# Attention, a Fourier mix and a feed-forward network on one core: three V slots, borrowed buffers, one batch's Fourier transform in f32, and a new order of the work

## The chip, the cores and the metric

The kernel runs on one core of one Trainium2 chip. The metric is the device time of one execution in microseconds (us); lower is better. The engines are TensorE (PE: matmuls and transposes; its weight loads are shown apart as PEld), VectorE (DVE), ScalarE (ACT), GpSimd (POOL) and SyncE (SP), which issues most of the DMA transfers.

## The reference

Eight batches of 576 positions, eight heads of 64. Attention sees a band of 64 positions; its output x is mixed by the real part of a two-dimensional Fourier transform, normalised, and run through a feed-forward network (512 to 2048 to 512) without biases:

```python
scores = (1 / sqrt(D)) * (q @ k.T)
mask = (rel >= 0) & (rel < 64)
attn = softmax(where(mask, scores, -1e9))
x = (attn @ v)                          # B x S x (H * D) = 8 x 576 x 512
u = x + real(fft(fft(x, axis=1), axis=2))
un = (u - mean(u)) / sqrt(var(u) + 1e-6)
out = u + relu(un @ w_ch1) @ w_ch2      # the weights come as 64-bit floats
```

## The kernel before, in words

**Tiles.** The 4,608 positions are 36 tiles T of 128 rows; nine tiles are a pair of batches. `attn_tile` loads K, Q and V of a tile, brings K and Q into transposed form, takes the scores of each 64-row half against its own and the previous 64 keys, subtracts the row minimum of the negated scores (DVE, tile `nm`), exponentiates (ACT, tile `pr`, the "P buffers"), transposes P (tile `pt`), multiplies with V (tile `pa` in PSUM) and normalises half a tile at a time into `xu` (`normed`, on DVE or on ACT as four activations). Then a radix-4 step over the columns and a transpose (`py`) collect a batch's rows in `yT`.

**Plain and split.** Tiles with T < `PRO` = 13 are "whole": they compute in f32, with PE transposes. Later ones are "split": each f32 number is a sum of two f16 numbers, and a product takes the three passes of `PASSES` (high x high, high x low, low x high); their transposes are DMA transposes. The first feed-forward chunk (`PLAIN` = 1) is in f32, the other 17 in split f16.

**Fourier transform.** `fft(b)` folds `yT` (DVE or POOL), forms three sums f and three h, splits each into high and low (`part`, `rest`), runs the first transform on PE against the constants `dd` (`dstage`, tiles `pg`, then `g`), the second against `ds_` (`sstage`, tile `pz`), mixes the two sides (`odd` on ACT, `mix` on DVE, tile `mp`) and sends the rows to memory (`send`). For batch 0 alone the rows of tiles 0 and 1 also go straight to the tiles `mt` (`direct`, 12 transfers). `norm_tile` gathers the rows (`mt`), adds them to `xu`, normalises and transposes into the FFN's input `uhl`.

**Weights.** 32 pieces of 512 KB (`weight_piece`) are loaded as 64-bit floats, made into f32 by three DVE operations, squared on ACT for a scale, and later split by `weight_split`. `Bwl` is a mark that all loads write, so that each load stands after the one before it.

**FFN.** `ffn(c)` takes two tiles at a time through 16 steps; each has a first product (`ph`, in the PSUM banks `f1`), ReLU on ACT and the remainder on DVE (`hh`), and a second product (`po`, in the two banks `f2`).

**The order.** No loop order decides what runs when. Every step is an `op` with an engine, an assumed duration, the buffers it reads and writes and a priority; `Plan.order` walks through a model of the engines, lets each take the ready step with the best start and priority, and the steps are issued in that order, each engine's queue then running in order. `RINGS` holds how many buffers of a kind there are. The tables `NUDGE`, `LEAD` and `BIAS` shift priorities and the choice between two engines, per kind of step, per place and per tile. Ahead of the first FFN matmul, wherever the model has PE waiting for more than 0.8, fill-in matmuls (`warm`) are issued, which compute nothing that is used:

```python
if early and o.eng == "PE" and gap > WARM[0]:
    for _ in range(int((gap - WARM[1]) / 0.21)):
        nc.tensor.matmul(warm, wide[:, 0:P], wide, start=True, stop=True)
```

**V.** Each 64-row half needs the keys' values of its own 64 rows and of the 64 before. Before, there are two buffers `va` for a tile's own rows and two `ve` for the rows before them; `v_own` copies the tile's upper half into its `ve` and `v_next` its lower half into the next tile's `ve`, two SBUF-to-SBUF transfers a tile (lines 624 and 632).

Of the kernel before, what the change touches and what calls it, by code (L numbers as in the profile page):

```python
# [12 lines left out]
F32 = mybir.dt.float32  # L13
F16 = mybir.dt.float16
# [39 lines left out]
PLAIN = 1  # L54
W_DMA, W_DMA_STEP, W_CONV, W_SQ, W_SPLIT, W_STEP = -30, 1.0, 40, 110, 60, 0.3
NUDGE = {
    "": (
        4.8, -0.5, 0, 4.7, -0.4, 23.1, 1.2, 18.3, -6.3, 3.3, 12.7,
    ),
    "even": (  # L60
# [12 lines left out]
    ),  # L73
    "part": (
        3, -3.6,
    ),
    "piece": (
        3.8, 0, -4.9, -12.5,
    ),
    "scale": (  # L80
        -7.5, -1.8, 30.2, 0, -0.8,
    ),
    "split": (
# [3 lines left out]
    ),  # L87
    "whole": (
        -1.6, -1.5, 14.9, 5.2, 0, 32.4, -0.2, 12.7, 3.6, -0.7, 0, -1.8, 0.6, 53.2, 1.4, -2,
        0, 0.4, -1.3, -1.6, -36.8, 3.3, -0.3, 5, 1.5, -1.3, -4.4, 0, -12.1, 2.1,  # L90
    ),
# [1342 lines left out]
```

## Time and profile before

| what | value |
|---|---|
| median of 3 runs | 999.92 us (998.57 to 1003.39) |
| the profiled execution, its own time | 1001.33 us |
| its span, first to last instruction | 999.6 us |
| mean granted clock of TensorE | 0.997 of full speed |
| busy: PE, DVE, ACT, POOL | 973.2, 678.3, 413.9, 158.9 us |
| matmul records, fill-in among them | 9083, 105 |
| data moved by DMA | 123.63 MB |

How to read it: busy time is the time in which an engine has an instruction running, over the whole span. Matmuls are pipelined and their ends are modelled, so a busy PE isn't PE at its peak. The "granted clock" is the share of TensorE's full speed. A wait is put down to what came last before the waiting instruction started. An f32 matmul that isn't a transpose makes two records in the trace, so 64 records are 32 matmuls.

### The profile page before, as it was taken

The page shows a single profiled execution, that of the slowest core. Times are in us where ns is not written, and L with a number is a line of the kernel's source. Part 1 is how long each engine was busy: PE and PEld are TensorE (multiplying, and loading weights), DVE is VectorE, ACT ScalarE, POOL GpSimd, SP SyncE. Part 2 cuts the span into 40 slices and gives each one's busy share as a digit, 9 for nine tenths or more (in the row PEclk, how much of TensorE's full clock was granted, in tenths as well). Part 3 has the DMA queues.
Part 4 walks back from the last instruction along what each step waited for, and adds up shares of the span by engine and source line. Part 5 has one row for each costly group of instructions (what it writes and reads, how often), then busy time and mean ns, then how long its engine had stood idle before and what let it go on. Part 6 is the DMA issues. An engine that isn't in the chain of part 4 may idle for free.

```text
span 999.6 us, 23005 instructions
## 1 busy us (share of the span) xinstructions
PE 973.2 (97%) x9083; PEld 684.4 (68%) x9083; DVE 678.3 (68%) x1810; ACT 413.9 (41%) x1141; POOL 158.9 (16%) x179
## 2 busy tenths in 40 slices
PE   8788999999999999999999999999999999999998
PEld 6666767676676667766676666766676667666664
DVE  4689898877878667787885578786875645542121
ACT  5667666755344344443452244442454212121111
POOL 0002101024112231231111221131013100200000
PEclk9999999999999999999999999999999999999999
DMA  9988975235647684878762575868665401330000
GB/s 212 225 216 214 238 198 131 67 70 125 136 118 166 139 161 99 182 163 147 156 120 67 124 176 110 177 123 159 130 139 113 95 12 45 58 71 23 1 22 22
DMA packets 310955, 123.63 MB, mean 124 GB/s; under 512 B 292728, under 2 KB 292856, under 8 KB 310848
## 3 DMA queue, kind: packets, MB, share of 16 engines
q1 hardware_dynamic: 308128, 113.25, 51.6%
q0 software_dynamic: 2720, 8.92, 3.4%
q8 instruction: 71, 1.16, 0.5%
q14 instruction: 36, 0.29, 0.1%
HBM read 54.99 MB, written 14.17 MB: 69 GB/s over the span
## 4 chain that ended last, share of the span: by engine, by line
PE 84%; DMA 6%; DVE 5%; ACT 2%; SPq 1%; issue 1%; POOL 0%; DVEq 0%; ACTq 0%; POOLq 0%
PE ph L1325 35%; PE po L1306 34%; PE pa L765 3%; PE pg L1001 2%; PE pz L1033 2%; PE psc L655 2%; DMA kn<-in_k 1%; DMA pt<-flex 1%; DMA mt<-md,gix 1%; DMA flex<-in_moe_w_ch 1%; PE warm L1405 1%; PE psc L669 1%; PE py L869 1%; PE pp L713 1%; DVE hh L1343 1%
## 5 line engine op out<-in xcount | busy, mean ns | idle before, releaser
L1325 PE MATMUL ph<-uhl,w0s 128*128 128x256 f16 (+1 forms) x3384 | 427.1, 277 | 3.8 <-DVE hh L1343 2.3
L1306 PE MATMUL po<-w1s,hh 128*128 128x512 f16 (+1 forms) x1696 | 425.9, 387 | 0.0
L1325 PEld LDWEIGHTS <-w0s 128*128 128x128 f16 x3264 | 317.5, 98 | 90.8 <-issue 8.0
L1340 ACT ACTIVATE hh<-ph 128x256 f16<-128x256 f32 x272 | 104.3, 384 | 423.4 <-PE ph L1325 351.2
L1343 DVE SCALAR_TENSOR_TENSOR hh<-ph,hh 128x256 f16<-128x256 f32 x272 | 114.6, 422 | 223.5 <-ACT hh L1340 203.1
L1306 PEld LDWEIGHTS <-hh 128*128 128x128 f16 x1632 | 155.7, 98 | 138.3 <-issue 0.2
L698 ACT ACTIVATE pr<-pr,nm 128x128 f32<-128x128 f32 x184 | 58.2, 392 | 4.0 <-DVE nm L689 4.0
L1135 POOL TENSOR_TENSOR rs<-mv,mhalf 128x1 f32<-128x1 f32 x36 | 23.6, 657 | 202.8 <-DVE mv L1131 190.8
L1111 POOL DMA_INDIRECT mt<-md,gix x34 | 37.3, 1098 | 100.9 <-DMA md<-mp 86.2
L727 POOL TENSOR_TENSOR flex<-pr,flex 128x512 f16<-128x512 f32 x27 | 33.5, 1242 | 110.5 <-ACT flex L491 69.9
L568 POOL TENSOR_TENSOR flex<-kn,flex 128x512 f16<-128x512 f32 x23 | 29.2, 1271 | 122.4 <-ACT flex L491 74.8
L780 ACT ACTIVATE xu<-pa,rc 128x64 f32<-128x64 f32 x152 | 35.0, 321 | 28.8 <-DVE rc L773 16.4
L689 DVE CUSTOM_DVE_ANT_0 pr<-psc,mskb 128x128 f32<-128x128 f32 x184 | 41.7, 284 | 2.8 <-PE psc L655 1.8
L765 PE MATMUL pa<-ve,pt 128*64 128x65 f16 (+1 forms) x760 | 39.7, 205 | 3.4 <-ACT pr L698 1.7
L765 PE MATMUL pa<-va,pt 128*64 128x65 f16 (+1 forms) x760 | 39.7, 205 | 0.6 <-DMA pt<-flex 0.5
L698 ACT ACTIVATE pr<-psc,nm 128x128 f32<-128x128 f32 x104 | 28.8, 387 | 6.4 <-DVE nm L687 6.2
L1033 PE MATMUL pz<-g,ds__76 97*96 97x257 f16 (+3 forms) x240 | 29.0, 273 | 0.5 <-DVE mp L1055 0.5
L1033 PEld LDWEIGHTS <-ds__76 97*96 97x96 f16 (+1 forms) x240 | 26.6, 124 | 2.5 <-DVE mp L1055 0.6
L655 PEld LDWEIGHTS <-qbd 128*64 128x64 f16 x736 | 21.6, 110 | 9.1 <-issue 9.0
L655 PE MATMUL psc<-kst,qbd 128*64 128x128 f16 x736 | 27.3, 221 | 0.0
L579 DVE TENSOR_TENSOR flex<-qn,flex 128x1024 f16<-128x1024 f32 x22 | 26.8, 1219 | 0.2
L1363 DVE SCALAR_TENSOR_TENSOR xu<-po,osc,xu 128x512 f32<-128x512 f32 x34 | 23.8, 742 | 3.7 <-PE po L1306 3.7
(162 smaller groups left out, 1121.8 us busy)
## 6 DMA issues: line engine op xcount, KB each, us to landing
wd<-in_moe_w_ch SPq DMA_DIRECT2D x20, 512.0 KB
out<-xu SPq DMA_DIRECT2D x36, 256.0 KB
ve<-va SPq DMA_DIRECT2D x67, 130.0 KB
kn<-in_k SPq DMA_DIRECT2D x32, 256.0 KB
qn<-in_q SPq DMA_DIRECT2D x32, 256.0 KB
flex<-in_moe_w_ch SPq DMA_DIRECT2D x12, 512.0 KB
flex<-in_v SPq DMA_DIRECT2D x20, 256.0 KB
md<-mp SPq DMA_DIRECT2D x24, 192.0 KB
```

What stands on the lines that cost most here:

```text
L655: nc.tensor.matmul(t["ps", x][64 * j : 64 * j + 64, hp], qbd[i][:, j, h, 64 * z : 64 * z + 64], keys(h, j), start=(z == 0), stop=(z == 1),)
L689: nc.vector.tensor_tensor_reduce(out=t["pr", jj][:, hp], in0=t["ps", jj][:, hp], in1=mskb[:, m : m + P], scale=-0.125, scalar=3.0e38, op0= ...
L698: nc.scalar.activation(pr, src, AF.Exp, bias=t["nm", jj][:, hp : hp + 1], scale=-1.0)
L727: eng.tensor_tensor(out=pp[:, :, 1], in0=t["pr", jj], in1=pp[:, :, 0], op=ALU.subtract)
L765: nc.tensor.matmul(pa[half_, hh], pt, v_, start=(x == 0), stop=(x == len(mm) - 1))
L780: nc.scalar.mul(xv[:, hh], pa[:, hh, 0:64], rc[:, hh])
L1033: nc.tensor.matmul(pz[:M, c0:c1], ds_[:NJ, a, c[0] : c[0] + c[1]], t["g", gi][:, b_, c0:c1], start=(x == 0), stop=(x == len(mm) - 1),)
L1111: nc.gpsimd.indirect_dma_start(out=mts[T], out_offset=None, in_=mds[pb][0 : HR if n < 4 else 2 * HR], in_offset=bass.IndirectOffsetOnAxis( ...
L1306: nc.tensor.matmul(t["po"][i], l_, r_, start=(f == 0 and x == 0), stop=(f == NKF - 1 and x == len(mm) - 1))
L1325: nc.tensor.matmul(ph, l_, r_, start=(x == 0), stop=(x == len(mm) - 1))
L1340: nc.scalar.activation(t["hh", f][:, 0], ph, AF.Relu)
L1343: nc.vector.scalar_tensor_tensor(out=hh[:, 1], in0=ph, scalar=0.0, in1=hh[:, 0], op0=ALU.max, op1=ALU.subtract)
```

## The change

- **V in three slots.** Tile T uses slot T mod 3 for its own rows. The slot of the tile before keeps its lower half and gets the new tile's upper half (`v_own`), and is then the `ve` of tile T: one copy a tile.
- **A second home for P.** For odd whole tiles the two P buffers and their two transposes lie in four sections of `flex` (`apart`), where weight pieces were loaded before; weight pieces now use `flex` only in one of its three pairs of sections (every fifth piece, before three of every seven).
- **Attention in the FFN's PSUM banks.** For T < `FREE` = 5 the product with V goes to `f2`.
- **K and Q.** Three buffers instead of two; tiles 1, 2 and 4 borrow those of `mp` and `g` (`KQ_AT`).
- **Batch 0's Fourier transform in f32.** `constants` adds the two f16 parts of `dd` and `ds_` into f32 tiles; `dstage` and `sstage` then take one f32 matmul in place of three f16 ones, and the splits into high and low are left out.
- **`direct`** is issued by ACT instead of SP.
- **Weight loads unchained:** a load no longer stands after the one before it; the mark `Bwl` is still read by what must come after all of them.
- **Order:** tile 5 counts among the early ones (`CUT`), new values in all tables, smaller `PATIENT`.

```diff
+FREE = 5
+KQ_AT = {1: "mp", 2: "g", 4: "mp"}
+CUT = 5
 NUDGE = {
     "": (
-        4.8, -0.5, 0, 4.7, -0.4, 23.1, 1.2, 18.3, -6.3, 3.3, 12.7,
+    "": {0: -0.7, 1: 2.2, 3: -9.2, 4: 11, 5: 2.6, 6: 0.1, 7: 1.1, 8: -3.1, 9: 10, 10: 1.3, 11: -1.3},
...
-    PATIENT = {"DVE": 0.25, "ACT": 0.5, "POOL": 0.75, "DMA": 0}
+    PATIENT = {"DVE": 0.1, "ACT": 0.25, "POOL": 0.75, "DMA": 0}
...
-        "kq": 2, "pr": 2, "pt": 2, "xu": XR, "y": 1, "yT": 1, "tail": 1,
+        "kq": 3, "pr": 2, "pt": 2, "xu": XR, "y": 1, "yT": 1, "tail": 1,
...
-    vbuf = [cp.tile([P, H * 65], F32, name=f"v{x}{i}") for x in "ae" for i in range(2)]
+    vbuf = [cp.tile([P, H * 65], F32, name=f"v{x}") for x in range(3)]
...
+        own, old = T % 3, (T + 1 if T == PRO else T - 1) % 3
...
         def v_own():
-            nc.sync.dma_start(vbuf[2 + i][0:64], vbuf[i][0:64])
-
-        def v_next():
...
-                nc.sync.dma_start(vbuf[3 - i][64:128], vbuf[i][64:128])
+            nc.sync.dma_start(vbuf[old][0:64], vbuf[own][0:64])
...
+        apart = whole and T % 2
+        prs = Bfl[0:2] if apart else [Buf("pr"), Buf("pr")]
...
+            at_ = "f2" if T < FREE else "ps"
+            bpa = Buf(at_)
...
+    def constants():
...
+                eng.tensor_tensor(out=whole_c[x], in0=src[:, 0, c0 : c0 + n], in1=src[:, 1, c0 : c0 + n], op=ALU.add)
+
+            op("POOL", 0.9, -39 + 0.01 * x, add, [Bdd if x < 2 else Bds], [Bc[x]], alt=("DVE", 0.45))
...
+        plain = b == 0
...
+                if plain:
+                    bfh[nm, r] = b3[r]
+                    continue
...
+                    for x, (s_, qq, c) in enumerate(terms if plain else ()):
...
+                        nc.tensor.matmul(to, s_[:, qq], w_, start=(x == 0), stop=(x == n - 1))
...
-                            nc.sync.dma_start(mts[T][r0 : r0 + 3 * (a1 - a0) - 2 : 3], t["mp", cl][a0:a1])
+                            nc.scalar.dma_start(mts[T][r0 : r0 + 3 * (a1 - a0) - 2 : 3], t["mp", cl][a0:a1])
...
-        w, more = {}, order % 7 - 4 if order % 7 > 3 else None
+        w, more = {}, 2 if order % 5 == 4 else None
...
-        op("DMA", 1.75, W_DMA + W_DMA_STEP * order, load, writes=[*bw, Bwl], lat=2.5)
+        Bwl.writers.append(op("DMA", 1.75, W_DMA + W_DMA_STEP * order, load, writes=bw, lat=2.5))
...
-        base = PITCH * T + (LATER if T > 4 else -EARLY)
+        base = PITCH * T + (LATER if T > CUT else -EARLY)
```

**Where the order moves.** First SP's queue near its start (`kn`, `qn`, `va` or `v`: loads of K, Q and V; `ve<-va` or `v<-v`: the copies; `wd`: a weight piece; `dd`: Fourier constants). Before:

```order
L516 DMA va0_81<-in_v 128x8x64
L516 DMA va1_82<-in_v 128x8x64
L516 DMA kn2_145<-in_k 128x8x64
L516 DMA qn2_172<-in_q 128x8x64
L632 DMA ve1_84<-va0_81 64x520
L624 DMA ve0_83<-va0_81 64x520
L453 DMA dd_75<-in_dft_d 128x1536
L516 DMA kn1_206<-in_k 128x8x64
L516 DMA qn1_221<-in_q 128x8x64
L624 DMA ve1_84<-va1_82 64x520
L1204 DMA wd0_0_249<-in_moe_w_ch1 128x1024
L632 DMA ve0_83<-va1_82 64x520
```

And with the change:

```order
L610 DMA v2_83<-v0_81 64x520
L497 DMA v1_82<-in_v 128x8x64
L497 DMA kn2_185<-in_k 128x8x64
L497 DMA qn2_198<-in_q 128x8x64
L497 DMA kn3_227<-in_k 128x8x64
L497 DMA qn3_244<-in_q 128x8x64
L497 DMA kn4_269<-in_k 64x8x64 x2
L610 DMA v0_81<-v1_82 64x520
L497 DMA v2_83<-in_v 128x8x64
L497 DMA qn4_329<-in_q 64x8x64 x2
L1238 DMA wd0_0_355<-in_moe_w_ch1 128x1024
```

Before, the first weight piece stands ahead of K and Q of tiles 3 and 4, and each tile has two copies; with the change K and Q of tiles 0 to 4 stand ahead of it, and each tile has one copy. Up to the load of K of tile 11, which PE needs just ahead of the first FFN matmul, SP issues with the change 17 weight pieces, 32 tiles' worth of K, Q or V and 8 copies.

Next the twelve `direct` transfers (`mt<-mp`). Before, they are in SP's queue:

```order
L1078 DMA mt0_1178<-mp0_1_1099 32x512
L1078 DMA mt0_1178<-mp0_1_1099 11x512
L1078 DMA mt1_1208<-mp0_1_1099 32x512
L1078 DMA mt1_1208<-mp0_1_1099 10x512
L1204 DMA flex_79<-in_moe_w_ch2 128x1024
L1061 DMA md0_1256<-mp0_1_1099 96x512
```

With the change they stand in ACT's queue between other work (`g`: the copy of the first transform's result; `pr`: exponentials; `mp`: one side of the mix):

```order
L1081 COPY mp0_2_962<-pz0_2_961 96x2
L1110 DMA mt1_998<-mp0_1_946 32x512
L1110 DMA mt1_998<-mp0_1_946 10x512
L1110 DMA mt0_1007<-mp0_1_946 32x512
L1110 DMA mt0_1007<-mp0_1_946 11x512
L471 ACTIVATE g0_0_985<-pg0_0_984 97x512
L471 ACTIVATE yT1_877<-py5_1010 128x4x128
L694 ACTIVATE pr6_0_911<-psc6_0_912,nm6_0_972 128x128 x4
```

A weight piece and the transfer to memory no longer stand behind them on SP; the copy for the third part of the transform, and the exponentials of tile 6, stand behind them on ACT.

Last DVE's queue in batch 0's Fourier transform, before (`fs`, `hs`: the split f16 numbers):

```order
L945 SCALAR_TENSOR_TENSOR f1_0_900<-f0_0_780,xe0_750 128x388
L950 TENSOR_TENSOR f0_0_780<-f0_0_780,xe0_750 128x388
L969 TENSOR_TENSOR fs1_0_905<-f1_0_900,fs1_0_905 128x388
L969 TENSOR_TENSOR fs0_0_907<-f0_0_780,fs0_0_907 128x388
L941 TENSOR_TENSOR h2_0_944<-yT0_298 128x388
L945 SCALAR_TENSOR_TENSOR h1_0_949<-h0_0_833,yT0_298 128x388
L950 TENSOR_TENSOR h0_0_833<-h0_0_833,yT0_298 128x388
```

And with the change:

```order
L960 SCALAR_TENSOR_TENSOR h1_0_852<-h0_0_760,yT0_377 128x388
L965 TENSOR_TENSOR h0_0_760<-h0_0_760,yT0_377 128x388
L960 SCALAR_TENSOR_TENSOR f1_0_862<-f0_0_734,xe0_701 128x388
L767 TENSOR_SCALAR rc5_0_890<-pa5_0_867 128x4
L770 RECIPROCAL rc5_0_890<-rc5_0_890 128x4
L965 TENSOR_TENSOR f0_0_734<-f0_0_734,xe0_701 128x388
```

The remainders `fs` and `hs` are gone; four additions for the f32 constants stand a little earlier in the queue. On PE, the fill-in matmuls ahead of the first FFN matmul are 62 in 12 runs where they were 105 in 19. Over the whole program ACT normalises 58 halves of attention output where it had 38, and DVE 14 where it had 34.

## Rows read from the trace of the kernel before

**Rows 1.** Stage: its us, busy PE, PEld, DVE, ACT, POOL, clock, DMA share, GB/s:
```profile
0.00:103.00 103.00, 85.40 (x1051) 68.72 (x1052) 74.02 (x169) 66.43 (x208) 7.95 (x21) 0.97 0.89 219
103.00:180.00 77.00, 76.96 (x543) 54.25 (x542) 66.80 (x144) 46.48 (x129) 7.77 (x7) 1.00 0.68 176
180.00:995.00 815.00, 810.33 (x7493) 561.47 (x7491) 536.18 (x1497) 301.01 (x806) 143.13 (x151) 1.00 0.50 107
```
**Rows 2.** The chain that ended last, by engine, whole span:
```profile
PE 84%; DMA 6%; DVE 5%; ACT 2%; SPq 1%; issue 1%; POOL 0%; DVEq 0%; ACTq 0%; POOLq 0%
```
**Rows 3.** Groups by line, PE, 0 to 102.76 us (busy us, mean ns, idle before):
```profile
L1405 PE MATMUL warm<-ident 128*128 128x256 f16 x105 | 17.8, 315 | 1.4 <-POOL va L457 1.4
```
**Rows 4.** PE's waits, 0 to 102.7 us (us in total, times, longest):
```profile
PE pk L553 <- DMA kn<-in_k: 2.1, 2, 1.9
PE pq L553 <- ACT xu L780: 1.9, 1, 1.9
```
**Rows 5.** Pieces of the chain of waits (start us, us, what):
```profile
30.13 2.68 PE py L869 x24
...
57.45 4.59 PE py L869 x24
...
67.53 1.13 PE pa L765 x32
...
70.35 2.12 PE pg L1001 x48
...
102.92 1.73 PE ph L1325 x8
...
164.58 2.63 PE pz L1033 x24
```
**Rows 6.** Timeline of SP, the twelve `direct` transfers (start us, us):
```profile
77.80 3.53 SPq L1078 DMA_DIRECT2D mt<-mp  x4
...
82.43 2.78 SPq L1078 DMA_DIRECT2D mt<-mp  x4
...
86.33 2.80 SPq L1078 DMA_DIRECT2D mt<-mp  x4
```
**Rows 7.** Busy time in two short stretches, columns as in rows 1:
```profile
56.00:60.00 4.00, 3.20 (x17) 2.97 (x18) 3.93 (x7) 3.67 (x14) 0.00 (x0) 0.71 0.82 216
...
75.00:100.00 25.00, 20.53 (x254) 15.98 (x253) 23.50 (x61) 18.30 (x65) 5.33 (x7) 0.93 0.82 215
```
**Rows 8.** Groups by line, DVE, 0 to 102.7 us:
```profile
L1011 DVE SCALAR_TENSOR_TENSOR g<-pg,g 97x512 f16<-97x512 f32 x3 | 2.0, 684 | 0.0
...
L969 DVE TENSOR_TENSOR fs<-f,fs 128x388 f16<-128x388 f32 x3 | 1.7, 562 | 0.1
L969 DVE TENSOR_TENSOR hs<-h,hs 128x388 f16<-128x388 f32 x3 | 1.6, 556 | 0.0
```
**Rows 9.** DMA, 0 to 103 us (issues: line, KB each):
```profile
DMA packets 38449, 22.57 MB, mean 219 GB/s; under 512 B 34051, under 2 KB 34179, under 8 KB 38436
...
wd<-in_moe_w_ch SPq DMA_DIRECT2D x12, 512.0 KB
flex<-in_moe_w_ch SPq DMA_DIRECT2D x7, 512.0 KB
...
ve<-va SPq DMA_DIRECT2D x17, 130.0 KB
```
**Rows 10.** Groups by line, ACT, 180 to 995 us:
```profile
L1340 ACT ACTIVATE hh<-ph 128x256 f16<-128x256 f32 x270 | 103.6, 384 | 422.3 <-PE ph L1325 351.2 <-PE po L1306 46.2 <-DVE hh L1343 18.7
...
L780 ACT ACTIVATE xu<-pa,rc 128x64 f32<-128x64 f32 x88 | 20.3, 319 | 14.7 <-DVE rc L773 9.0 <-PE pa L765 3.1 <-DVE rc L770 2.5
```
**Rows 11.** PE's waits, 103 to 996 us:
```profile
PE ph L1325 <- DVE hh L1343: 2.3, 6, 0.8
PE ph L1325 <- ACT hh L1340: 1.3, 2, 0.7
```

More of the change, by code (lines that the diff above doesn't have):

```diff
@@ L231, in op @@
         o = Op()
-        shift, lead = NUDGE.get(self.kind, ()), LEAD.get({"split": "whole", "odd": "even"}.get(self.kind, self.kind), ())
-        prio += (shift[self.k] if self.k < len(shift) else 0.0) + (lead[self.at] if self.at < len(lead) else 0.0)
+        lead = LEAD.get({"split": "whole", "odd": "even", "first": "even"}.get(self.kind, self.kind), ())
+        prio += NUDGE.get(self.kind, {}).get(self.k, 0.0) + (lead[self.at] if self.at < len(lead) else 0.0)
         o.group = (self.kind, self.at, self.k)
@@ L441, in attn_fft_ffn_kernel @@
     Bid, Bmh, Bmskb, Bgix, Bdd, Bds, Bones = (Buf() for _ in range(7))
-    Bq, Bva, Bve = ([Buf() for _ in range(2)] for _ in range(3))
+    Bq = [Buf() for _ in range(2)]
+    Bv = [[Buf(), Buf()] for _ in range(3)]
     BkT = [Buf() for _ in range(3)]
@@ L619, in attn_tile @@
         if not whole:
-            op("ACT", 0.52, base + 3, lambda: v_part(0), [bv], [Bva[i]])
-            op("DVE", 0.6, base + 3.1, lambda: v_part(1), [bv], [Bva[i]])
+            op("ACT", 0.52, base + 3, lambda: v_part(0), [bv], Bv[own])
+            op("DVE", 0.6, base + 3.1, lambda: v_part(1), [bv], Bv[own])
         def v_own():
-            nc.sync.dma_start(vbuf[2 + i][0:64], vbuf[i][0:64])
-        def v_next():
-            if T + 1 == PRO:
-                (hi, lo), v_ = (ve[1 - i][64:128, z] for z in range(2)), va32[i][64:128]
+            nc.sync.dma_start(vbuf[old][0:64], vbuf[own][0:64])
@@ L629, in v_next, with v_tail @@
+        was = plan.k
+        if T == PRO:
+            last = (T - 1) % 3
+            plan.begin("tail", T)
+            plan.k = 1
+            def v_tail():
+                (hi, lo), v_ = (va[old][64:128, z, :, 0:64] for z in range(2)), va32[last][64:128, :, 0:64]
                 nc.vector.tensor_scalar(out=hi, in0=v_, scalar1=VS, scalar2=None, op0=ALU.mult)
                 nc.vector.scalar_tensor_tensor(out=lo, in0=v_, scalar=VS, in1=hi, op0=ALU.mult, op1=ALU.subtract)
-            else:
-                nc.sync.dma_start(vbuf[3 - i][64:128], vbuf[i][64:128])
@@ L634, in attn_tile @@
-        op("DMA", 0.55, base - 4 if whole else base + 3.2, v_own, [Bva[i]], [Bve[i]], lat=2.8)
-        if n + 1 < NT and T + 1 == PRO:
-            op("DVE", 1.1, base + 6, v_next, [Bva[i]], [Bve[1 - i]])
-        elif n + 1 < NT:
-            op("DMA", 0.55, base - 3.9 if whole else base + 6, v_next, [Bva[i]], [Bve[1 - i]], lat=2.8)
+            if n == 0:
+                op("POOL", 0.7, base - 25, lambda: nc.gpsimd.memset(va[old][64:128, :, :, 0:64], 0.0), writes=[Bv[old][1]])
+            else:
+                op("DVE", 1.1, base + 0.3, v_tail, [Bv[last][1]], [Bv[old][1]])
@@ L640, in attn_tile, with quarter @@
+            part_ones(last)
+            plan.begin("split", T)
+        plan.k = was
+        op("DMA", 0.55, base - 4 if whole else base + 3.2, v_own, [Bv[own][0]], [Bv[old][0]], lat=2.8)
         m = P * (1 if n == 0 else 2 if n == 4 else 0)
         banks = [Buf("ps"), Buf("ps")]
-        prs = [Buf("pr"), Buf("pr")]
+        apart = whole and T % 2
+        prs = Bfl[0:2] if apart else [Buf("pr"), Buf("pr")]
         rd = [Bq[i], bkT, *([] if n == 0 else [BkT[before]])]
+        def quarter(x):
+            return flex[:, x].rearrange("p (a s) -> p a s", a=4)
@@ L743, in attn_tile, with av @@
         Bx[T] = bx
-        vts = (ve32[i], va32[i]) if whole else (ve[i], va[i])
+        vts = [(va32 if whole else va)[x] for x in (old, own)]
         for hf in range(2):
-            bpa = Buf("ps")
-            def av(hf=hf):
+            at_ = "f2" if T < FREE else "ps"
+            bpa = Buf(at_)
+            def av(hf=hf, at_=at_):
                 if hf == 0:
                     xts[T] = sb([P, DM], F32, "xu", f"xu{T}")
-                pa = t["pa", hf] = bank("ps", f"pa{T}_{hf}", (P, 4, 65))
+                pa = t["pa", hf] = bank(at_, f"pa{T}_{hf}", (P, 4, 65))
                 for hh in range(4):
@@ L930, in fft @@
             b1, b0_ = low[0][bsrc], low[-1][bsrc]
-            b3 = [Buf("r3") for _ in range(3)]
+            r3 = "fh" if plain and x else "r3"
+            b3 = [Buf(r3) for _ in range(3)]
             def view(src):
```

181 lines of the change are left out of this document (98 added, 83 removed), and 10 rows, old and new, of the table NUDGE.

## The prediction

> **What bounds the kernel now.** I first read TensorE's share of the span by stage, then the chain of waits, then each engine's waits inside the first stage. TensorE (PE in the rows) is busy for 76.96 of 77 us from 103 to 180 us and for 810.33 of 815 us from 180 to 995 us [rows 1], and the chain that ended last is 84% PE [rows 2]. So after about 103 us the time is the sum of PE's work, and whatever is saved must either be PE work or lie before 103 us, where the feed-forward part (FFN) starts: its first matmul on PE's queue begins close to 102.9 us [rows 5]. Until 103 us PE is busy for 85.40 us, so it idles for 17.6 us [rows 1], and of its busy time 17.8 us are the 105 fill-in matmuls that the program sets wherever its order foresees a gap, and that compute nothing [rows 3]. Together 35.4 us of the first 103 us are no work. The idle part has many small causes, none over 2.1 us in total: loads of keys, then a normalisation on ACT, and so on down [rows 4]. Behind them DVE is busy for 23.50 of 25 us from 75 to 100 us and ACT for 18.30 [rows 7], and the DMA engines move 22.57 MB by 103 us, 219 GB/s [rows 9]. No single engine bounds this stage: it is a chain through PE, ACT, DVE and the loads, with all of them nearly full towards its end.
>
> A measurement of this kernel can tell about 0.5% (5 us) from no change. The profiled execution took 1001.33 us, its span 999.6 us plus 1.7 us around it; the median of the runs is 999.92 us, 1.4 us lower. The sum is made against 1001.33 us, and 1.4 us is taken off at the end.
>
> **The change part by part.**
>
> *Fewer fill-in matmuls.* The changed order has 62 of them ahead of the first FFN matmul where there were 105, in 12 runs instead of 19; the first three runs (18, 2 and 2) are the same. One costs 17.8 / 105 = 0.17 us [rows 3], so 43 fewer are 7.3 us less on PE. **-7.3 us**, certain as work, but only gone from the time if no wait takes its place; that is the next term.
>
> *Idle time around them.* PE idled for 17.6 us in this stage [rows 1]; 1.4 us of it is the start [rows 3], the same in both. The other 16.2 us lay around 16 runs of fill-in, and the change has 9 such runs. In proportion to the runs 16.2 x 7/16 = 7.1 us go. What removes them is visible in the order: the loads for tiles 0 to 4 now stand ahead of the first weight load on SP, since keys and queries have a third buffer and three borrowed homes, so that PE's 2.1 us of waits for keys [rows 4] should go; P buffers of odd tiles and the attention output of tiles 0 to 4 no longer queue for the same slots. Bounds: by the matmuls themselves (83 to 40 after the common start) 16.2 x 43/83 = 8.4 us go; if all waits only move, 0. I take **-7.1 us**, since a run marks a wait better than its length does.
>
> *Batch 0's Fourier transform in f32.* It had 72 matmuls for the first transform and 30 for the second, in three f16 passes: 2.12 x 72/48 = 3.2 us and 2.63 x 30/24 = 3.3 us, 6.5 us on PE [rows 5]. In f32 there are 24 and 10, with 2,304 and 2,560 columns. Wide f32 matmuls cost 1.73 us for 4 of 256 columns, 1.69 ns a column; the narrow f32 ones of the attention output cost 1.13 us for 8 pairs of 65 columns, 2.2 ns a column [rows 5]. The f32 transform so takes 4,864 x 1.69 = 8.2 us to 4,864 x 2.2 = 10.7 us, 1.7 to 4.2 us more. The first transform has narrow pieces (63 to 128 columns), the second wide ones: 2,304 x 2.2 + 2,560 x 1.69 = 9.4 us. **+2.9 us**. On DVE six remainders of 0.56 us and three of 0.68 us go, 5.4 us [rows 8]; four additions that build the f32 constants come, near 0.56 us each by the remainders, whose width is about the same, 2.2 us. These 3 us of DVE, in the stretch where it is fullest, help the waits of the term above to shrink; they are not counted twice.
>
> *One V copy instead of two, three slots.* SP issues 17 V copies of 130 KB by 103 us [rows 9]; up to the last load that the first FFN matmul stands behind (keys of tile 11) the changed order has 8. Counting the issues up to that point, 20.5 MB must be issued where before it was about 23.0 MB; at the 219 GB/s of [rows 9] that is 93.5 us. So the loads alone allow an FFN start near 93 us, and an earlier one only at a higher rate. This part adds no term, it sets the floor on which the other terms are checked.
>
> *The twelve rows of the Fourier result for tiles 0 and 1, issued by ACT instead of SP.* On SP the three groups of four took 3.53, 2.78 and 2.80 us, 9.1 us, with the next weight load and the transfer to memory queued behind them [rows 6]. ACT has never issued a DMA in this trace, so its price is bounded: 0 if ACT only passes them on, 9.1 us if each holds ACT as it held SP. Queued behind them on ACT are the copy of the last Fourier piece, for which PE's last transform of the batch waits, the exponentials of tile 6 and the P copies. ACT idles for 25 - 18.30 = 6.7 us from 75 to 100 us [rows 7]; what doesn't fit there is 9.1 - 6.7 = 2.4 us. I take **+2.4 us**, nearer to the lower end, because SP's freed 9.1 us also bring the weights and the Fourier rows out earlier. The Trainium skill says in "DMA: Bandwidth & Descriptors", section "Issuing engines are not separate DMA queues", that starting transfers from several engines saves only the sequencer's time, which it calls "usually small relative to the DMA itself". By that rule this term would be 0 and the sum 2.4 us lower. On SP the trace disagrees: 9.1 / 12 = 0.76 us an issue.
>
> *Unchained weight loads, one pair of flex sections instead of three for them, tile 5 early.* These only change the order; they are priced by the fill-in count and the byte count. What covers them is that 19 weight loads were issued by 103 us [rows 9], and 17 are by the corresponding point now, of which the first FFN steps need the first. If that cover failed, the first chunk's FFN would wait for weights, and PE would idle after 93 us, where it idled 0.04 us in 77.
>
> *The steady part.* PE's instructions after the FFN start are the same work; PE waits there for ACT and DVE only 2.3 + 1.3 us [rows 11] and idles 4.7 us in all [rows 1]. I take no change, with 4.7 us either way as bound.
>
> **Sum.** -7.3 - 7.1 + 2.9 + 2.4 = -9.1 us, so 992.2 us for a profiled execution and **991 us** as a median. The FFN would start near 102.9 - 9.1 = 93.8 us, just where the byte count allows it. The ends: -7.3 - 8.4 + 1.7 + 0 = -14.0 us and, with the steady part's idle time gone, -18.7 us (981 us as a median); and -7.3 + 0 + 4.2 + 9.1 = +6.0 us (1006 us as a median), where every unknown falls badly.
>
> **The rivals.**
>
> 1. *The waits only move* (loads or ACT): the 43 fill-in matmuls become idle time. For it: the DMA engines are busy for 0.89 of this stage [rows 1] and DVE for 94% of its end. Against it: 2.5 MB fewer bytes to issue and 3 us less DVE work. Then the +2.9 and +2.4 us stay and of the 14.4 us gained none to a half: 998 to 1005 us as a median. Its other form is TensorE's clock: from 56 to 60 us the granted clock was 0.71 on average, which mixes 2.4 and 1.2 GHz, after PE had idled, and a block of 24 transposing matmuls took 4.59 us instead of 2.68 us [rows 5, 7]. With fewer fill-ins each remaining wait could bring that back, 1.9 us a time; three more such drops make 6 us, 997 us. The Trainium skill's page "TensorE: Matmul & The Clock Gate", section "HAM oscillation — how this bites in real kernels", says that waits in front of matmuls make the clock fall back each time. The drop at 56 us agrees with it.
> 2. *Deeper gain*: with SP free of the 9.1 us and fewer V copies the loads run faster than 219 GB/s, all waits shrink by 8.4 us and the steady idle by half: -14.0 - 2.4 = -16.4 us, 984 us (979 to 987).
> 3. *Slower: normalisations on ACT.* The new order gives ACT 58 half-tiles of the attention output to normalise where it had 38, 21 of the extra ones in the steady part by the counts after the FFN start. Each is four activations, 20.3 x 4/88 = 0.92 us [rows 10], and stands ahead of the FFN's activations, for which the next matmuls wait. If each held PE for its whole 0.92 us, that is +19.3 us, and 1001.3 - 9.1 + 19.3 - 1.4 = 1010 us. It makes the kernel slower by over 0.5% from 15 of the 21 on ((9.1 + 5) / 0.92). Against it: ACT waited 351.2 us for PE in that place, not PE for ACT [rows 10, 11].
> 4. *The change doesn't act*: V's three slots or the second homes might only shift which transfer is waited for, and the tables might restore the old start. About 1000 us.
>
> **How the numbers follow.** My forecast (987 to 995 us) gets 0.5, the deeper gain 0.2, the moved waits in both forms 0.2 (a fifth of that below 995 us, since part of a wait may still go), the slower case 0.06, no effect 0.04. The forecast's own ends and the rivals' give a range of 981 to 999 us; left out are the slower case, and the outer edges of the others. Faster by over 0.5% means below 994.9 us: 0.5 + 0.2 + 0.04 = 0.74. Within 0.5%: 0.20. Slower: 0.06.
>
> **What would show it.** Right: the fill-in matmuls near 10.5 us, PE's first FFN matmul at 92 to 95 us, PE idle before it near 10 us, and from there on PE busy without gaps as before. The f32 transform should show 9 to 10 us on PE. On ACT's queue the twelve DMA issues show their price directly; if each takes 0.7 us and exponentials start late behind them, the +2.4 is too small. Wrong: an FFN start after 98 us, or over 10 us of idle time after it, or half-clock stretches in front of it.

## The result and the profile after

The changed kernel takes **992.06 us** (median of 6 runs, 989.48 to 993.59) beside 1000.72 us of the kernel before (6 runs, 998.57 to 1004.21): a ratio of 0.9909, 95% interval 0.9884 to 0.9933. It is 0.9% faster, 1.1 us from the predicted 991.0 us and inside the range. The profiled execution took 992.03 us, its span 990.2 us.

The view of busy time in stretches, now of the changed kernel (columns as in [rows 1]); the first stretch ends where the feed-forward part (FFN) starts:

```profile
0.00:93.14 93.14, 79.60 (x968) 63.32 (x969) 66.27 (x150) 60.19 (x191) 10.18 (x24) 0.98 0.90 230
93.14:990.20 897.06, 886.86 (x8040) 616.08 (x8038) 576.54 (x1596) 374.80 (x1040) 180.37 (x183) 1.00 0.51 109
...
63.00:80.00 17.00, 11.29 (x123) 8.82 (x121) 11.12 (x28) 8.00 (x27) 0.00 (x0) 0.90 0.87 258
...
72.00:76.00 4.00, 3.17 (x30) 2.27 (x34) 2.55 (x5) 3.15 (x7) 0.00 (x0) 0.58 1.00 313
```

The same two stretches of the kernel before:

```profile
0.00:102.76 102.76, 85.16 (x1050) 68.51 (x1051) 74.02 (x169) 66.19 (x208) 7.95 (x21) 0.97 0.89 219
...
102.76:999.60 896.84, 888.00 (x8036) 615.93 (x8034) 604.26 (x1641) 347.73 (x934) 150.90 (x158) 1.00 0.52 113
```

So in these two executions the whole difference lies ahead of the FFN start, which moved from 102.76 to 93.14 us, 9.6 us earlier. What follows takes 896.8 us before and 897.1 us now. In the first stage TensorE (PE) idles for 93.14 - 79.60 = 13.5 us where it was 17.6 us. Of the idle time that is left, 5.7 us lie between 63 and 80 us, and there the granted clock falls once (0.58 from 72 to 76 us, a mean of its two levels, 1.2 and 2.4 GHz).

The group of the fill-in matmuls, to be set beside [rows 3]:

```profile
L1440 PE MATMUL warm<-ident 128*128 128x256 f16 x62 | 10.2, 307 | 1.3 <-POOL mhalf L430 1.3
```

PE's timeline (start us, us, what) with the f32 transform of batch 0 ([rows 5] has its f16 pieces) and the first FFN matmul:

```profile
50.76 0.95 PE L1017 MATMUL pg<-c,f 128*97 128x65 f32 x8
51.55 0.95 PE L1017 MATMUL pg<-c,h 128*97 128x63 f32 x8
52.33 1.03 PE L709 MATMUL pp<-ident,flex 128*128 128x128 f32 x8
...
55.59 1.02 PE L1017 MATMUL pg<-c,f 128*97 128x65 f32 x8 [0.53 <-DVE f L960]
...
59.52 3.69 PE L1057 MATMUL pz<-g,c 97*96 97x257 f32 x16
63.05 0.95 PE L1017 MATMUL pg<-c,f 128*97 128x65 f32 x8
...
67.44 1.11 PE L1057 MATMUL pz<-g,c 97*97 97x257 f32 x4 [1.78 <-ACT g L471]
68.38 0.60 PE L535 MATMUL pk<-ident,kn 128*128 128x128 f32 x4
...
93.14 1.89 PE L1359 MATMUL ph<-uhl,w0s 128*128 128x256 f32 x8
```

Read from start to start, one f32 `pg` stage takes 52.33 - 50.76 = 1.57 us, three of them 4.7 us, and the `pz` stages 63.05 - 59.52 = 3.5 us and 68.38 - 67.44 = 0.94 us: 9.2 us. The first `pg` starts at 50.8 us, where it was 70.4 us [rows 5].

PE's waits ahead of the FFN start (us in total, times, longest), beside [rows 4]:

```profile
PE pk L535 <- ACT xu L777: 2.3, 1, 2.3
PE pz L1057 <- ACT g L471: 1.8, 1, 1.8
PE pq L535 <- DMA qn<-in_q: 1.6, 3, 1.0
```

The keys are gone from the list; two single waits for ACT now lead it. ACT's timeline (columns as PE's, in brackets the idle time before) shows what stood ahead of the second, the DMA issues of `direct`:

```profile
63.34 0.66 ACTq L1110 DMA_DIRECT2D mt<-mp  x1
64.04 2.70 ACTq L1110 DMA_DIRECT2D mt<-mp  x3
66.78 0.60 ACT L471 ACTIVATE g<-pg 97x512 f32<-97x512 f32 x1 [3.04 <-issue]
...
69.38 2.77 ACTq L1110 DMA_DIRECT2D mt<-mp  x4
72.20 0.58 ACT L471 COPY pt<-pp 128x512 f32<-128x512 f32 x1 [2.91 <-DVE w1s L1247]
...
74.82 0.53 ACTq L1110 DMA_DIRECT2D mt<-mp  x1
...
75.90 2.20 ACTq L1110 DMA_DIRECT2D mt<-mp  x3
```

The copy of `g` starts at 66.78 us, and PE's `pz`, which needs it, at 67.44 us. The five rows hold ACT for 8.9 us in three stretches. The planner, the program's model of the engines, charges 0.15 us and a fixed 0.1 us for a pair of transfers.

### The profile page after: what moved, and what is told of

It is laid out like the page before. It is cut to its first block, busy times and chain, and to the rows that moved or that the text cites. A ratio compares the mean times of both kernels' runs of the same rounds, so it can differ in the third digit from the quotient of the medians.

```text
span 990.2 us, 22890 instructions
## 1 busy us (share of the span) xinstructions
PE 966.5 (98%) x9006; PEld 679.4 (69%) x9006; DVE 642.8 (65%) x1745; ACT 435.0 (44%) x1230; POOL 190.6 (19%) x207
## 3 DMA queue, kind: packets, MB, share of 16 engines
q1 hardware_dynamic: 305232, 108.60, 50.8%
## 4 chain that ended last, share of the span: by engine, by line
PE 84%; DVE 4%; DMA 3%; ACT 1%; issue 1%; ACTq 0%; SPq 0%; DVEq 0%; POOL 0%
PE ph L1359 37%; PE po L1340 36%; PE pa L762 3%; PE pz L1064 2%; PE psc L651 2%; PE pg L1025 2%; DMA qbd<-flex 1%; DMA mt<-mp 1%; DVE hh L1377 1%; PE py L871 1%; PE pp L709 0%; DVE pr L685 0%; PE psc L665 0%; DMA mt<-md,gix 0%; DVE st L1160 0%
## 5 line engine op out<-in xcount | busy, mean ns | idle before, releaser
L723 POOL TENSOR_TENSOR flex<-pr,flex 128x512 f16<-128x512 f32 x46 | 57.0, 1244 | 165.4 <-ACT flex L471 144.7
L777 ACT ACTIVATE xu<-pa,rc 128x64 f32<-128x64 f32 x232 | 51.5, 324 | 27.0 <-DVE rc L770 15.9
L762 PE MATMUL pa<-v,pt 128*64 128x65 f16 (+1 forms) x1328 | 32.0, 201 | 0.2
L471 ACT CAST flex<-pr 128x512 f16<-128x512 f32 x43 | 26.1, 615 | 3.1 <-DMA pt<-flex 3.0
L801 DVE TENSOR_TENSOR y<-xu 128x256 f32<-128x256 f32 x58 | 23.8, 452 | 5.4 <-ACT xu L777 5.3
L762 PEld LDWEIGHTS <-pt 128*64 128x64 f16 x1104 | 19.9, 111 | 9.3 <-issue 8.9
L1359 PEld LDWEIGHTS ph<-uhl,w0s 128*128 128x128 f32 x120 | 22.1, 190 | 5.5 <-issue 2.8
L1160 DVE BATCH_NORM_STATS2 st<-xu 128x6 f32<-128x512 f32 x36 | 25.0, 695 | 1.2
L1064 PE MATMUL pz<-g,ds__76 97*96 97x257 f16 (+3 forms) x210 | 25.8, 273 | 0.0
```

Source lines behind the costliest of these rows:

```text
L723: eng.tensor_tensor(out=pp[:, :, 1], in0=t["pr", jj], in1=pp[:, :, 0], op=ALU.subtract)
L762: nc.tensor.matmul(pa[half_, hh], pt, v_, start=(x == 0), stop=(x == len(mm) - 1))
L777: nc.scalar.mul(xv[:, hh], pa[:, hh, 0:64], rc[:, hh])
L1064: nc.tensor.matmul(pz[:M, c0:c1], ds_[:NJ, a, c[0] : c[0] + c[1]], t["g", gi][:, b_, c0:c1], start=(x == 0), stop=(x == len(mm) - 1),)
L1359: nc.tensor.matmul(ph, l_, r_, start=(x == 0), stop=(x == len(mm) - 1))
```

## The experiments

All runs in one table. "Start" is the first FFN matmul in the profiled execution, "rest" the span less the start. Each ratio is to the kernel before in the same session, with its 95% interval. "Start" and "rest" are of one execution each: for e2, e4, e5, e7 and e12 it is the fastest that was measured of its kernel, for e3 and e10 the slowest.

| kernel | median us | ratio | start | rest |
|---|---|---|---|---|
| before | 1000.72 | 1 | 102.76 | 896.8 |
| changed | 992.06 | 0.9909 [0.9884, 0.9933] | 93.14 | 897.1 |
| e1 `direct` on SP | 992.86 | 0.9928 [0.9916, 0.9940] | 94.53 | 895.7 |
| e2 `direct` on POOL | 988.14 | 0.9888 [0.9873, 0.9902] | 89.73 | 895.9 |
| e3 before, `direct` on ACT | 1005.03 | 1.0051 [1.0038, 1.0064] | 106.64 | 897.6 |
| e4 no fill-ins | 994.51 | 0.9961 [0.9943, 0.9978] | 91.85 | 898.0 |
| e5 changed, empty tables | 1008.02 | 1.0074 [1.0055, 1.0093] | 96.31 | 906.8 |
| e6 before, empty tables | 1010.25 | 1.0090 [1.0069, 1.0111] | 103.59 | 905.3 |
| e7 more copies | 993.12 | 0.9932 [0.9914, 0.9951] | 92.42 | 896.6 |
| e8 POOL, planned anew | 1000.13 | 0.9996 [0.9981, 1.0011] | 93.65 | 904.4 |
| e9 more fill-ins | 995.20 | 0.9950 [0.9931, 0.9969] | 93.37 | 899.7 |
| e10 before, no fill-ins | 1000.86 | 1.0010 [0.9997, 1.0023] | 104.32 | 896.9 |
| e11 DVE work back | 997.07 | 0.9973 [0.9955, 0.9991] | 97.63 | 897.1 |
| e12 e2 and a later weight load | 990.02 | 0.9909 [0.9886, 0.9932] | 90.29 | 896.7 |

The theory that I set out with (A): the time is the FFN start plus some 897 us, the gain is fewer waits ahead of the start, and ACT held by `direct` is the largest one left. Its rivals: the loads' bytes set the start (B), or the new tables alone make the gain (C).

### Who issues the twelve transfers: e1, e2, e3

```diff
-                            nc.scalar.dma_start(mts[T][r0 : r0 + 3 * (a1 - a0) - 2 : 3], t["mp", cl][a0:a1])
+                            nc.gpsimd.dma_start(mts[T][r0 : r0 + 3 * (a1 - a0) - 2 : 3], t["mp", cl][a0:a1])
```

That is e2; e1 has `nc.sync` in that place. In e3 the kernel before gets `nc.scalar` where it had `nc.sync`. The order of all instructions stays.

> The changed kernel, its order of work untouched, but the twelve direct transfers are issued by SP at the same places. In the changed kernel they held ACT for 8.8 us between 63 and 78 us, where PE idles 5.7 us. Theory A (ACT being held is what is left of the waits): ACT is free of that, PE idles 2 to 4 us less before the FFN starts, the FFN starts at 89 to 91 us, and the time is 2 to 4 us below the changed kernel's 992 us, at about 0.987 of the kernel before. Theory B (the loads bound the first stage, and SP is their queue): 9 us of issue in front of the loads delay them, the FFN starts at 95 to 100 us, 0.994 to 1.000 of before.

> The changed kernel, order untouched, the twelve direct transfers issued by GpSimd, which does nothing in that stretch. Theory A: as on SP or better, since neither ACT nor the loads' queue is held: FFN start 88 to 91 us, 0.984 to 0.988 of the kernel before. Theory B: the loads are where they were, so the start stays at 93 us and the time at 0.991, give or take 0.002. If GpSimd needs over 1 us an issue, the rows of tiles 0 and 1 arrive later and part of the gain of theory A goes.

> The kernel before with this one edit: the twelve direct transfers are issued by ACT, the order untouched. The forecast's +2.4 us term alone. Theory A: ACT is held for about 9 us at 77 to 89 us, where it idled a quarter of the time: 1 to 6 us slower, 1.001 to 1.006 of before. If an issue were cheap on ACT, or SP's held queue were what cost: 1 to 4 us faster, 0.996 to 0.999.

The group of these issues in e1 and in e2 (durations in ns: least, median, most; first and last start in us), the time from issue to landing in e2, and then e2's stretch from 63 to 80 us:

```profile
L1110 SPq DMA_DIRECT2D mt<-mp x12: 535/670/894, 62.3 to 75.4; - x12
```
```profile
L1110 POOL DMA_DIRECT2D mt<-mp x12: 501/518/782, 62.2 to 70.0; - x12
...
DMA to landing us min/median/max: 4.9/5.5/6.0
```
```profile
63.00:80.00 17.00, 13.38 (x158) 10.22 (x157) 12.53 (x31) 12.11 (x38) 6.81 (x13) 0.90 0.91 282
```

No queue issues them for nothing: 0.72 us a transfer (median) on ACT, 0.67 on SP, 0.52 on POOL. What differs is who stands behind. POOL had no other work in this stretch; with the transfers there ACT is busy for 12.11 us from 63 to 80 us where it was 8.00, PE idles for 3.6 us instead of 5.7, and FFN starts 3.4 us earlier. On SP the loads of queries stand behind them, and among PE's waits of e1 these loads now lead:

```profile
PE pq L535 <- DMA qn<-in_q: 5.9, 4, 2.6
```

So e1 fits neither expectation as written (89 to 91, or 95 to 100 us): SP instead of ACT frees ACT, holds the loads, and starts FFN 1.4 us later, with ratios whose intervals overlap. In the kernel before, whose order was made for SP, ACT as the issuer costs 3.9 us of the start and 0.5% of the time. So holding ACT costs 3.4 us of the start beside an idle POOL in the one kernel, and 3.9 us beside SP in the other; beside SP in the changed kernel, whose order was made for ACT, it costs nothing that can be seen. That e2 beats e1 is clear from the intervals. That it beats the changed kernel is only likely: 3.9 us by the medians, 2.1 us by the ratios, and the intervals overlap.

### Are fill-ins work on the path? e4, e9, e10

```diff
-                for _ in range(int((gap - WARM[1]) / 0.21)):
+                for _ in range(int((gap - WARM[1]) / 0.21 * 1.55 + 0.5)):
```

That is e9; e4 has `range(0)` there, and e10 has `range(0)` in the kernel before.

> The changed kernel without its 62 fill-in matmuls, order untouched. Leaves out nothing of the result. If they only lie in waits: their 10.2 us become idle time, the FFN starts at 93 us, the time is 0.991 of before within 0.002. If they keep TensorE's clock up, as the forecast's second form of rival 1 has it: more stretches below full clock in front of the FFN, 2 us each, 0.993 to 1.000 of before. If they were themselves the path: up to 10 us faster, 0.981.

> The changed kernel with 42 more fill-in matmuls, 104 where it had 62 and where the kernel before had 105, in the same places (each run longer by about two thirds); all else in the same order. If fill-ins are work on the path, as the term of -7.3 us took them, 42 x 0.17 = 7.1 us come back: start of the feed-forward part at 100 us, time near 999 us. If they lie in time in which TensorE would wait anyway, the start moves by less than 2 us, the idle time before it shrinks by about 5 us or more, and the time stays at 991 to 994 us.

> The kernel before without its 105 fill-in matmuls, order of all else untouched. If they are work on the path, all but the first 1.4 us of their 17.8 us go, less what a lower clock costs: start of the feed-forward part at 90 to 95 us, time 985 to 993 us. If they lie in waits, as removing the 62 from the changed kernel gave nothing, the start stays within 3 us of 102.8 us, PE's idle time before it grows from 17.6 us to 28 us or more, and the time is 997 to 1004 us.

The first stage of e9, of e4 and of e10, columns as in [rows 1]:

```profile
0.00:93.37 93.37, 83.62 (x1010) 67.58 (x1011) 66.22 (x150) 60.49 (x191) 10.20 (x24) 0.98 0.91 229
```
```profile
0.00:91.85 91.85, 74.76 (x907) 58.63 (x908) 66.65 (x151) 60.13 (x191) 10.19 (x24) 0.96 0.95 233
```
```profile
0.00:104.32 104.32, 76.37 (x944) 61.91 (x945) 74.43 (x170) 66.09 (x208) 7.95 (x21) 0.92 0.89 217
```

With 42 more (e9) PE is busy 4.0 us longer and idles 9.75 us instead of 13.5; the start moves by 0.2 us. e9's time is 0.4% above the changed kernel's by the ratios, with intervals that touch. Its profile puts 2.7 us behind the start: PE is busy there for 888.54 us where it was 886.86, and at 668 us, at the end of a wait of 2.6 us for FFN's input, the clock falls:

```profile
668.00:672.00 4.00, 3.78 (x22) 2.83 (x23) 2.07 (x5) 1.51 (x3) 0.00 (x0) 0.60 0.88 228
```

Why that wait was longer (1.9 us in the changed kernel, without a fall of the clock) is open. Without any fill-ins, the rest of PE's work grows. Subtracting the fill-ins' busy time overstates this, since the record of a fill-in overlaps those of its neighbours. Counted record by record, a matmul other than a fill-in runs for 70.9 us of the first stage of the kernel before and for 76.4 us in e10, 5.5 us more; it is 71.9 us in the changed kernel and 74.8 us in e4, 2.8 us more. The granted clock falls from 0.97 to 0.92 and from 0.98 to 0.96 in these stretches. Taken as full-speed time that is missing, this is (1 - 0.92) x 104.32 = 8.3 us beside 3.1 us, and 3.7 beside 1.9 us: 5.2 and 1.8 us more, which is enough for nearly all of the first growth and most of the second. So a fill-in takes time in which PE would wait anyway, and buys back clock; taking all away changes the start by -1.3 us (e4) and +1.6 us (e10), and the time by nothing (e10) or for the worse (e4: 0.5% by the ratios, with intervals that do not overlap). e4's profiled execution is its fastest, 991.63 us beside a median of 994.51 us, so that its start of 91.85 us is not the usual one.

### Do the bytes of the loads set the start? e7

```diff
             nc.sync.dma_start(vbuf[old][0:64], vbuf[own][0:64])
+            if T < 9:
+                nc.sync.dma_start(dr.tile([64, H * 65], F32, tag=f"vx{T}", name=f"vx{T}"), vbuf[own][64:128])
```

> The changed kernel with one further transfer of 130 KB beside the V copy of tiles 0 to 8, from the V slot to a scratch in the chip's memory that nobody reads: nine transfers, 1.2 MB, issued by SP where the V copies are issued, the order of all else as it was. That is about what the change took out of the first stage. If the bytes of the loads set the feed-forward start (20.5 MB at 219 to 234 GB/s), 1.2 MB is 5.1 to 5.5 us: the start goes from 93.1 to about 98.5 us and the time from 992 to 997 us. If the first stage is a chain through TensorE, ACT and DVE in which the loads are early enough, the start stays within 1.5 us and the time within 2 us.

DMA ahead of the FFN start, in the changed kernel and in e7:

```profile
DMA packets 39596, 21.44 MB, mean 230 GB/s; under 512 B 35840, under 2 KB 35968, under 8 KB 39585
```
```profile
DMA packets 39719, 22.49 MB, mean 243 GB/s; under 512 B 35387, under 2 KB 35515, under 8 KB 39708
```

1.05 MB more were moved by a start that came 0.7 us earlier; the mean rate rose with the demand. The first stage of e7:

```profile
0.00:92.42 92.42, 79.39 (x969) 62.96 (x970) 66.26 (x150) 60.25 (x191) 10.19 (x24) 1.00 0.96 243
```

The clock never fell in it, where the changed kernel's fell once (0.98 of 93.14 us, 1.9 us of full-speed time), so the copies may have cost a microsecond that this hides. The 5.1 to 5.5 us that bytes as the limit would have added are far from it, and the median rose by 1.1 us. Theory B falls as a matter of bytes. Single late loads still count (e1).

### Structure or tables? e5, e6, e8

```diff
-NUDGE = {
...
-}
+NUDGE, LEAD, BIAS = {}, {}, {}
```

This is done to the changed kernel (e5) and to the one before (e6). e8 is e2 with the planner told of it: `op("POOL", 1.0, ...)` for `op("ACT", 0.15, ...)`, tables as they were.

> The changed kernel with its three tables of order (NUDGE, LEAD, BIAS) empty, so that the planner sets the order by its own priorities; buffers, f32 Fourier and weight chaining stay as changed. It is to be set beside the kernel before with its own tables empty. If the buffers and the loads are what made the gain, this kernel is 5 to 15 us faster than that one; if the gain lies in the rows of the new tables, the two are within 3 us of each other. Both should be slower than with their tables, by 5 us or more, since a late feed-forward start and waits of TensorE after it are what the tables move. The planner sets 63 fill-in matmuls here.

> The kernel before with its three tables of order empty. The planner sets 115 fill-in matmuls where it set 105, so it foresees about the same gaps; the start of the feed-forward part should be at 103 to 115 us and the time 1000 to 1030 us. What decides is the distance to the changed kernel with empty tables: 5 to 15 us if the structure makes the gain, under 3 us if the tables do.

> The changed kernel with the twelve transfers of the Fourier rows issued by POOL, and the planner told so, at 1.0 us for each pair where it was told 0.15 us on ACT; so the order is a new one, and the tables were not made for it. The planner sets 56 fill-in matmuls where it set 62. If the time follows from the waits before the feed-forward start, and the planner uses the freed ACT, this is as fast as the version in which only the queue was changed (988.1 us) or up to 3 us faster, start at 87 to 90 us. If the tables fit only the order for which they were made, the start comes 2 us later or more and the time is over 991 us.

e5 from the FFN start to 985 us, with PE's longest wait there, and then e6 in the same two views:

```profile
96.31:985.00 888.69, 872.45 (x7892) 606.82 (x7889) 606.29 (x1631) 355.54 (x989) 160.76 (x156) 1.00 0.50 109
```
```profile
PE ph L1312 <- DMA uhl<-up: 7.2, 2, 5.8
```
```profile
103.59:985.00 881.41, 872.22 (x7927) 606.14 (x7927) 593.92 (x1617) 365.74 (x1023) 147.31 (x146) 1.00 0.53 114
```
```profile
PE ph L1257 <- DVE hh L1275: 4.7, 5, 1.7
```

Both readings hold a part. In the profiles the structure alone starts FFN 7.3 us earlier (96.31 beside 103.59). But the medians lie only 2.2 us apart, with overlapping intervals; the criterion written down beforehand (under 3 us) decides for the tables. Part of the difference is that e5 idles for 16.2 us behind its start, 7.2 of them in waits for the transposed input of FFN, where e6 idles for 9.2 us. The rest is that e5's profiled execution is the fastest of its four (1004.88 us; the others took 1007.5 to 1009.0), so that the 7.3 us are not typical of it. The tables are worth 16.0 us in the changed kernel (1008.02 to 992.06) and 9.5 us in the one before, most of it behind the start. e8 says how tightly they fit: an order planned with a truer price loses all that the queue alone had won and the change's whole gain besides (0.9996), 3.9 us of it ahead of the start and 8.5 us behind (904.4 beside e2's 895.9). What the change gained thus needs tables that were made for its order; how much of the gain is the buffers' and how much the tables', these runs do not separate.

### The f32 transform's other side: e11

Seven DVE steps of batch 0's transform are done twice, four of them ahead of the first transform and three between the two, where the f16 remainders had been:

```diff
-                eng.tensor_tensor(out=t[nm, which], in0=up, in1=dn, op=al)
+                for _ in range(2 if plain and eng is nc.vector else 1):
+                    eng.tensor_tensor(out=t[nm, which], in0=up, in1=dn, op=al)
...
                 copy(eng, t["g", r] if plain else t["g", r][:, 0], t["pg", r][:NJ], 1.0 / YS)
+                if plain:
+                    copy(nc.vector, t["g", r], t["pg", r][:NJ], 1.0 / YS)
```

The step `mid` is doubled in the same way.

> The changed kernel with seven of VectorE's (DVE's) steps of batch 0's Fourier transform done twice, in the places where the kernel before had its f16 remainders: four sums of 0.56 us and, for the three pieces between the two transforms, one more scaling copy each by DVE behind ACT's, near 0.68 us; 4.3 us of DVE work in all, the order of all else untouched. The change took 5.4 us of remainders from DVE there and added 2.2 us. If this relief of DVE (and the step that PE no longer waits for between the transforms) made part of the earlier feed-forward start, the start goes from 93.1 to 95.5 us or later, the time from 992 to 994.5 us or more, and PE's waits for f and g grow. If DVE has room there, both stay within 1.5 us.

PE's timeline of e11 at the second `pg` and the last `pz`, the stretch that holds the latter, and the whole first stage (columns as in [rows 1]):

```profile
57.78 1.60 PE L1019 MATMUL pg<-c,f 128*97 128x65 f32 x8 [2.52 <-DVE f L962]
...
72.10 2.02 PE L1061 MATMUL pz<-g,c 97*97 97x257 f32 x4 [2.67 <-DVE g L473]
```
```profile
72.00:76.00 4.00, 3.90 (x14) 3.28 (x15) 3.53 (x10) 1.34 (x7) 0.00 (x0) 0.50 0.37 90
...
0.00:97.63 97.63, 84.65 (x968) 68.26 (x969) 71.16 (x158) 60.23 (x191) 10.56 (x24) 0.93 0.89 220
```

In the changed kernel these matmuls waited 0.53 and 1.78 us, and the `pz` block took 1.11 us; here it takes 2.02 us after its wait, at a granted clock of 0.50, the lower level of 1.2 GHz. The start comes 4.5 us later, and the time rises by 0.6% with intervals that do not overlap. So DVE's chain through this transform is on the changed kernel's path: 4.3 us more of DVE work cost 4.5 us. They don't show as idle time, which is 97.63 - 84.65 = 13.0 us beside 13.5. They show as slower matmuls: PE is busy 5.1 us longer with the same 968 records, and the clock of the stage is 0.93 where it was 0.98, (1 - 0.93) x 97.63 = 6.8 us of full-speed time beside 1.9. The two waits grew by 2.0 and 0.9 us, and the clock fell behind both. The executions say the same: the two of e11 whose mean clock was 0.998 took 993.85 and 994.92 us, the ten others, at 0.991 to 0.996, 996.5 to 1001.9 us. How much the DVE work would cost at full clock was not measured by itself.

### One load later: e12

In e2's order the weight load of piece 11 is moved on SP, from behind the queries of tile 8 to behind the keys of tile 9:

```diff
+        i, j = at["piece", 11, 0], at["whole", 9, 0]
+        seq.insert(j, seq.pop(i))
```

> The changed kernel with the twelve transfers of Fourier rows issued by POOL (988.1 us, start of the feed-forward part at 89.7 us), and with one weight load of 512 KB (piece 11) issued by SP two places later, behind the keys of tile 9 where it stood behind the queries of tile 8. The queries of tile 8 were issued at 64.1 us and took 6.3 us to land while that weight load ran beside them, and TensorE, which idles 2.6 us up to 70.5 us, goes on just as they land. If what counts is when single loads land, not the sum of the bytes, they land by 69 us, the start comes 1 to 2 us earlier and the time is 986 to 987.5 us. If the load is slow because the twelve transfers themselves fill the DMA queues, nothing moves by more than 0.7 us.

The DMA view of the queries' tile, and PE's timeline:

```profile
DMA to landing us min/median/max: 5.8/5.8/5.8
```
```profile
70.47 0.63 PE L535 MATMUL pq<-ident,qn 128*128 128x128 f32 x4 [2.18 <-DMA qn<-in_q]
```

The queries, issued at 64.5 us, still landed at 70.3 us, and the start came 0.6 us later, inside the 0.7 us of the second expectation. The neighbouring weight load is not what makes them slow, so the first expectation falls. The median is 1.9 us higher, 0.2% by the ratios, with intervals that overlap. Whether the twelve transfers fill the queues, as the second had it, was not tried by itself and stays open.

## Why the prediction was right, and where not

**What bounds the kernel: right.** Over all kernels with tables in the order that they were made for, the start ranges from 89.7 to 106.6 us, while the rest stays at 895.7 to 898.0 us (e9, 899.7, is the exception). The forecast start was 93.8 us, the measured one 93.14.

**Fewer fill-ins, -7.3 us: the count was right, but it is no term of its own.** 62 fill-ins took 10.2 us, as foreseen (10.5). But e9 and e10 show that fill-ins are no work on the path: they fill waits. The step that failed is adding them to the idle time as a saving of its own, "certain as work". Only the sum of both can be priced: it was 17.8 + 17.6 = 35.4 us and is 10.2 + 13.5 = 23.7 us, 11.7 us less, where the two terms said 14.4.

**Idle time around them, -7.1 us: too much.** It fell by 4.1 us, to 13.5 us where near 10 was expected. What I had named as gone (keys) is gone; in its place are single waits behind ACT's DMA issues.

**The f32 transform, +2.9 us: right on PE, incomplete on the path.** PE's share went from 6.5 to 9.2 us, +2.7. DVE's relief had no term of its own, only the remark that it helps the waits. e11 shows that it can count: PE waits for DVE's steps ahead of and between the two transforms, and 4.3 us more of them cost the changed kernel 4.5 us, largely by way of the clock. That the same relief made the gain is not shown. In the kernel before, the chain of waits up to the FFN start (pieces as in [rows 5]) has of DVE's steps that were left out only the two on `fs`, 0.84 us, and 27 us of loads of keys, V and weight pieces:

```profile
10.27 4.09 DMA kn<-in_k
...
23.58 5.79 DMA kn<-in_k
...
34.46 5.52 DMA va<-in_v
...
43.63 7.65 DMA flex<-in_moe_w_ch
...
54.40 0.28 DVE fs L495
...
54.71 0.56 DVE fs L969
...
81.37 3.90 DMA flex<-in_moe_w_ch
```

The new buffers and the new order concern such loads. How much each of the buffers, the order and DVE's relief does was not separated.

**`direct` on ACT, +2.4 us: depends on the order.** The term was ACT in place of SP. In the order of the kernel before it is +3.9 us of the start (e3); in the changed order, made for ACT, it is -1.4 us (e1), within the noise of the ratios. The 3.4 us of e2 are against POOL, not SP. I had written that at 0.7 us an issue the term would be too small; it is 0.72 us, and all prices lie below the bound of 9.1. The Trainium skill ("DMA: Bandwidth & Descriptors", section "Issuing engines are not separate DMA queues") calls the time that it takes an engine's sequencer to start a transfer usually small beside the transfer itself. The trace agrees with that, 0.52 us beside 5.5 us to landing in e2; that the term is then 0 doesn't follow, since what stands behind the issues waits for them (e3).

**The byte floor of 93.5 us: the number came out, the reason did not.** e7 moved more by an earlier start, and e2 started at 89.73 us. A mean rate of a stage in which the queues also wait is not a limit.

**The steady part, 0: right**, 896.8 and 897.1 us. PE idles in it for 10.2 us to the end, a little over the 10 us that I had named as a sign of being wrong; but in the kernel before it idles there for 8.8 us. With it rival 3 falls (the 21 more normalisations on ACT were not felt), and so does the strong form of rival 1. Its clock form showed in the other direction: the clock of the first stage rose from 0.97 to 0.98, one drop was left, and e11 shows what more of them cost. The Trainium skill ("TensorE: Matmul & The Clock Gate", section "HAM oscillation — how this bites in real kernels") says that long enough waits for data between groups of matmuls make the clock fall back, each time anew. e11's 0.50 behind a wait of 2.67 us agrees; that not every wait does so, e7 shows, where the clock stayed at 1.00 ahead of the start with a wait of 2.5 us for ACT in it. Of the deeper gain of rival 2 (984 us) e2's 988.1 us is a part, by another queue than the one I had thought of.

So the 991 us rest on terms that erred against each other, and that they came within 1.1 us is in part luck. Against 9.1 us foreseen the start moved by 9.6: the fill-ins and idle time are 11.7 us less where 14.4 were foreseen, and the rest of PE's time, by subtraction 79.60 - 10.2 = 69.4 beside 85.16 - 17.8 = 67.4 us, is 2.0 us more where +2.9 and +2.4 us were.

## What to carry to other kernels

Price fill-ins and idle time as one quantity, and look behind it for the chain that feeds the waiting engine: e11 found a part of it on DVE, which is busy for only 66.27 of 93.14 us. Look at the clock too: a wait can cost more through the matmuls behind it than by itself (e11). Each of these DMA issues held its engine for half a microsecond or more; put them on one that has nothing queued behind it, and give the planner their true length before its tables are made, since tables made for one order are lost on another (e8).

## What the runs showed of the hardware

The same twelve transfers held their issuer for 0.72 us (ACT), 0.67 us (SP) and 0.52 us (POOL) each at the median, and up to 1.28 us on ACT and 1.32 us on SP in the kernel before. The mean rate of the DMA engines was no constant of the stage: 219 GB/s in the kernel before, 230 in the changed one, 243 when more was asked for. And the fill-ins' use can be read from the clock: without them it was 0.92 instead of 0.97 in the first stage of the kernel before, and the same matmuls took 5.5 us longer; in the changed one it was 0.96 instead of 0.98, and they took 2.8 us longer.
